# A third seven-product unit in the first product of the last two token tiles, interleaved product by product, with the sums of x taken one tile ahead

## The chip, the cores and the metric

The kernel runs on one core of a Trainium2 chip. The metric is the time of one execution on the device in microseconds. Where a profile is read, PE is the matrix engine (PEld its weight loads), DVE the vector engine, ACT the scalar engine, POOL and SP the two other engines, which here only issue transfers and do small set-up work. Each engine takes its instructions strictly in the order in which the program gave them, and waits at an instruction whose inputs or output buffer are not ready.

## The reference

Attention over pooled keys and values, and then a two-layer network with a SiLU between:

```python
k_p = k.reshape(B, H, Sp, 8, D).mean(axis=3); v_p = the same of v      # B = H = 8, S = 576, Sp = 72, D = 64
attn = softmax(q @ k_p.T / sqrt(D));  x = (attn @ v_p) as [4608, 512]
h = x @ w_in            # 512 -> 2048
g = h / (1 + exp(-h))   # SiLU
out = g @ w_out         # 2048 -> 512
```

All inputs and the output are float32; the kernel multiplies in bfloat16 and accumulates in float32.

## The kernel before

The 4608 tokens are worked in nine tiles of 512 (t = 0 to 8). A tile has two stages, written one after the other in the loop at the end of the kernel: `up` (the first product and the SiLU: x times `w_in` into `h_T`) and `down_quarters` (the second product: `h_T` times `w_out` into the output; tile 0 uses the plain `down`). The attention of batch t + 1 (scores, exponentials, denominators, numerators, and the multiplication that writes x into `xT`) is done in pieces inside tile t, and is over when tile 6 ends: tiles 7 and 8 hold only the two products.

There is no scheduler. The order on every engine is that in which the Python code runs. Each stage walks through its matmuls and calls `next(step)` before each; `spread` runs a *filler*, a small function with a due step, as soon as that step has been reached. Fillers of the first product are put into `f_up`, those of the second into `f_down`. A filler that is due at step n is issued behind the matmul of step n. Steps of `up` count one plain matmul of 512 tokens or two matmuls of 256 each; steps of `down_quarters` count one matmul (7 products of 16, 112 in all).

*The first product.* The 2048 hidden columns are 16 groups of 128. A plain group (`plain`, line 541) is four matmuls of 128x512 that accumulate in one bank, and a SiLU on ACT (line 547). Two *units* of four groups each, groups 4 to 7 and 8 to 11, are computed instead as a 2x2 block product by the seven-product method (Strassen's: seven block products of sums instead of eight of blocks). A product (`product`, line 482) is four matmuls of 128x256. The seven products use three banks P, Q and R, and are combined as they come (`stage`): 2 into P, copied by ACT into `r_sb` (line 499); 5 into Q, added on DVE to `r_sb`, giving `rr_sb` (line 502); 1 into R, from which DVE makes `t_sb` (line 505); 4 added into P and 3 added into Q, each taken by a SiLU on ACT straight from its bank; then 7 added into P and 6 added into Q, each added on DVE to `t_sb` into `c_sb[0]` and `c_sb[1]` (lines 514 and 517), which the SiLUs "h" and "s" read (line 490). So product 6 may only be issued after the SiLU of product 3 has read bank Q, and product 7 after that of product 4. `r_sb`, `rr_sb`, `t_sb` and the two `c_sb` exist once and are shared by all units. Sums of weights (`w_sum1`, five for each unit, line 442) are made once in tile 0; sums of x (`x_sum`, five for each tile, line 449) are made at the start of each tile's `up`.

In tiles 2 to 8 the order is: plain groups 12 and 13, products 2 5 1 of the first unit, group 14, products 4 3, group 15, products 7 6, and so on through the second unit with groups 0 and 1 between, ending with group 2, the SiLU s of the second unit, and group 3.

*The second product* is one seven-product unit over the whole tile. Its left operands are sums of quarters of `h_T` (`hidden_sum`, line 609, on DVE), each made in two halves of 128x1024: the half over groups 4 to 7 and 12 to 15 first, the half over groups 0 to 3 and 8 to 11 after. The order of its matmuls follows: products 2 and 5 over the first halves, products 2 and 5 over the second halves, then products 1, 4, 3, 7, 6. Product 1 needs both halves of `h_sum` 1.

PSUM has eight banks: three are handed out in turn under the tag "mm" (plain groups, R of a unit, and P, Q, R of the second product), five under "at" (scores, denominators, numerators, and P and Q of a unit). A tile that takes a bank waits until the last reader of the bank's tile before it is done. In tiles 2 to 6 `down_quarters` holds, in order: at step 56 one bank of denominators, then four of numerators, which four multiplications on DVE read (line 398); at step 75 four banks of scores (line 345), whose sixteen matmuls go round the four banks in turn; at step 97 denominators and two banks of numerators, at step 101 two more of these in tile 6.

DVE in tile 6's `down_quarters` does, in order: `rr_sb`, `hidden_sum(7)` (step 33, line 609, 128x2048), `t_sb` (line 668), four multiplications of line 398, `hidden_sum(6)` (step 71), the copy of bank Q (line 676), the addition from bank P (line 680), four more multiplications, the addition from bank Q (line 684), and then, as first work of tile 7, the five sums of x.

Of the kernel before, what the change touches and what calls it, by code (L numbers as in the profile page):

```python
# [27 lines left out]
FP32 = mybir.dt.float32  # L28
FP32R = mybir.dt.float32r
BF16 = mybir.dt.bfloat16  # L30
AX = mybir.AxisListType.X
AF = mybir.ActivationFunctionType
ALU = mybir.AluOpType
# [3 lines left out]
def kernel(  # L37
# [9 lines left out]
    nc = tc.nc  # L47

    B, H, S, D = q.shape
# [11 lines left out]
    KQ, NQ, CQ = KG // 2, NTT // 2, d_model // 2  # L61
# [20 lines left out]
    singles = ctx.enter_context(tc.tile_pool(name="singles", bufs=1))  # L82
# [8 lines left out]
    def ps_tile(shape, dtype, tag, name):  # L91
        return psum.tile(shape, dtype, tag=tag, bufs=banks[tag], name=name)
# [18 lines left out]
    t_sb = singles.tile([128, 2, CQ], FP32, name="t_sb")  # L111
    xT = singles.tile([128, KF, NX], BF16, name="xT")

    w_sum1 = [singles.tile([128, 5, 2, 256], BF16, name=f"w_sum1{n}") for n in range(2)]
    x_sum = singles.tile([128, 5, 2, NQ], BF16, name="x_sum")
    c_sb = [singles.tile([128, 2, NQ], FP32, name=f"c_sb{n}") for n in range(2)]

# [206 lines left out]
    def third(n):  # L324
        return tuple((g, n * QV, (n + 1) * QV) for g in range(2))
# [50 lines left out]
    def numerators(b, segs, tags=("at", "at")):  # L376
        st = batches[b]
        w = width(segs)
        g0, i0, i1 = segs[0]
        c0 = b * S % NX + i0 * QP  # L380
        cols = slice(c0, c0 + (i1 - i0) * QP)
        es = st.pop(("es", segs))
        rec = st.pop(("rec", segs))
        nu = []
        for c in range(2):
            nu_ps = ps_tile([128, 512], FP32, tags[c], "nu_ps")
            for g, _, _, cs in seg_cols(segs):
                for s in range(4):
                    nc.tensor.matmul(  # L389
                        nu_ps[32 * s : 32 * (s + 1), cs],  # L390
                        lhsT=st["vp"][:, 4 * g + s, c::2],
                        rhs=es[:, s, cs],
                        start=True, stop=True,
                    )
            nu.append(nu_ps)
        ng = len(segs)
        for c in range(2):
            nc.vector.tensor_mul(  # L398
                out=xT[:, 2 * g0 + c : 2 * (g0 + ng - 1) + c + 1 : 2, cols],
                in0=nu[c][:, :w].rearrange("r (g n) -> r g n", g=ng),  # L400
                in1=rec.rearrange("r (g n) -> r g n", g=ng),
            )
# [4 lines left out]
    def moe_tables():  # L407
        nc.scalar.preload_act_table_set("silu_and_others")
# [10 lines left out]

    UNITS = ((4, 6), (8, 10))
    UW = [
        {
            (i, j): w_in_sb[:, 2 * j : 2 * j + 2, 128 * u : 128 * (u + 2)]
# [7 lines left out]
    U_WI = {n: i for i, n in enumerate(U_W)}  # L433
# [6 lines left out]
    def unit_weight_sum(y, n):  # L440
        a, b = U_W[n]
        nc.vector.tensor_tensor(
            out=w_sum1[y][:, U_WI[n]], in0=UW[y][a], in1=UW[y][b],
            op=ALU.subtract if n in (6, 7) else ALU.add,
        )

    def unit_x_sum(t, n):
        a, b = U_X[n]
        nc.vector.tensor_tensor(
            out=x_sum[:, U_XI[n]], in0=x_quarter(t, *a), in1=x_quarter(t, *b),  # L450
            op=ALU.subtract if n in (3, 4) else ALU.add,
        )

    def unit_weights(y, n):
        if n in U_WI:
            return w_sum1[y][:, U_WI[n]]
        return UW[y][0, 0] if n == 3 else UW[y][1, 1]

    def unit_x(t, n):
# [5 lines left out]
    def up(t, fillers, items):  # L465
        step = spread(
            fillers,
            sum(
                KF if len(it) == 3 else 2 * len(it[1].strip("hs")) for it in items
            ),  # L470
        )
        ps = {}

        def product(y, n, bank, first):
            if first:
                tag = "mm" if bank == "R" else "at"
                ps[bank] = ps_tile([128, 2, NQ], FP32, tag, f"u_ps{bank}")
            w, x = unit_weights(y, n), unit_x(t, n)
            for u in range(2):
                next(step)  # L480
                for kk in range(2):
                    nc.tensor.matmul(  # L482
                        ps[bank][:, u, :], lhsT=w[:, kk, 128 * u : 128 * (u + 1)],
                        rhs=x[:, kk, :], start=first and u == 0 and kk == 0,
                        stop=kk == 1, skip_group_check=True,
                    )

        def hidden(y, i, j, src):
            g = UNITS[y][i]
            nc.scalar.activation(  # L490
                h_T[:, g : g + 2, j * NQ : (j + 1) * NQ], src, func=AF.Silu
            )

        tt = nc.vector.tensor_tensor

        def stage(y, n):
            if n == "2":
                product(y, 2, "P", True)
                nc.scalar.copy(r_sb, ps["P"])
            elif n == "5":  # L500
                product(y, 5, "Q", True)
                tt(out=rr_sb, in0=ps["Q"], in1=r_sb, op=ALU.add)
            elif n == "1":
                product(y, 1, "R", True)
                tt(out=t_sb, in0=ps["R"], in1=rr_sb, op=ALU.subtract)
            elif n == "4":
                product(y, 4, "P", False)
                hidden(y, 1, 0, ps["P"])
            elif n == "3":
                product(y, 3, "Q", False)  # L510
                hidden(y, 0, 1, ps["Q"])
            elif n == "7":
                product(y, 7, "P", False)
                tt(out=c_sb[0], in0=ps["P"], in1=t_sb, op=ALU.add)  # L514
            elif n == "6":
                product(y, 6, "Q", False)
                tt(out=c_sb[1], in0=ps["Q"], in1=t_sb, op=ALU.add)
            elif n == "h":
                hidden(y, 0, 0, c_sb[0])
            else:  # L520
                hidden(y, 1, 1, c_sb[1])

        for it in items:
            if len(it) == 3:
                plain(t, step, *it)
            else:
                for n in it[1]:
                    stage(it[0], n)
        for _ in step:
            pass  # L530
# [75 lines left out]
    def hidden_sum(n, k0, k1):  # L606
        a, b, op = H_SUMS[n]
        ks = slice(k0, k1)
        nc.vector.tensor_tensor(  # L609
            out=h_sum[n][:, ks, :], in0=quarter(*a, ks), in1=quarter(*b, ks), op=op  # L610
        )
# [167 lines left out]
    def load_half_2(name, half):  # L779
        for i0, i1 in ((0, SA), (SA, SLOTS), (SLOTS, SLOTS + 1)):  # L780
            load_slots(nc.gpsimd, 2, name, i0, i1, half)

    visits = [third(n) for n in range(3)]
    for t in range(NT):
        a = t + 1
        f_up, f_down = [], []
        if t == 0:
            GA = 11
            items = [(g, 0, HS) for g in range(GA)]
            items += [(g, HS, NTT - HS) for g in range(GA)]  # L790
            items += [(g, 0, NTT) for g in range(GA, KG)]
            f_up += [(1, lambda: denominators(0, part(0, 1), on_dve=True))]
            f_up += [(5, lambda: denominators(0, part(1, 1), on_dve=True))]
            f_up += [(13, lambda: numerators(0, part(0, 1)))]
            f_up += [(17, lambda: numerators(0, part(1, 1)))]
        else:
            G = lambda *gs: [(g, 0, NTT) for g in gs]
            if t == 1:
                items = (
                    G(12, 13, 14, 15) + [(0, "251")] + G(8) + [(0, "43")] + G(9)  # L800
                    + [(0, "7h6")] + G(10) + [(0, "s")] + G(11, 0, 1, 2, 3)
                )
            else:
                items = (
                    G(12, 13) + [(0, "251")] + G(14) + [(0, "43")] + G(15) + [(0, "76")]
                    + [(1, "2")] + [(0, "hs")] + [(1, "51")] + G(0) + [(1, "43")] + G(1)
                    + [(1, "7h6")] + G(2) + [(1, "s")] + G(3)
                )
            for n in U_X:
                f_up.append((0, lambda n=n: unit_x_sum(t, n)))  # L810
            for n in (2, 5):
                f_up.append((36 if t > 1 else 45, lambda n=n: hidden_sum(n, 4, 8)))
            f_up.append((56, lambda: hidden_sum(6, 4, 8)))
            for n, k0 in ((2, 0), (5, 0), (1, 4), (1, 0)):
                f_up.append((64, lambda n=n, k0=k0: hidden_sum(n, k0, k0 + 4)))
            f_down.append((33, lambda: hidden_sum(7, 0, 8)))
            f_down.append((71, lambda: hidden_sum(6, 0, 4)))
# [9 lines left out]
        if a < B:  # L827
# [50 lines left out]
            for n, sg in enumerate(visits):  # L878
                if n < 2 or not 0 < t < B - 2:
                    f_down.append((nu_at[n], lambda sg=sg: numerators(a, sg)))  # L880
                if n == 0 and 1 < t < B - 1:
                    f_down.append((nu_at[n], lambda: numerators(a - 1, visits[2])))
        moe_tables()
        up(t, f_up, items)
        if t == 0:
# [31 lines left out]
```

The softmax here doesn't subtract the row's maximum and nothing guards it: scores larger than these inputs give would overflow.

## Time and profile before

| | |
|---|---|
| median of four runs | 285.43 us (285.37 to 285.48) |
| the profiled execution | 285.24 us, of which the profile's span is 283.3 us |
| granted TensorE clock | 1.0 in all of the span |
| PE busy | 277.1 us, 98% of the span |
| DVE busy | 225.5 us, 80% |
| ACT busy | 183.5 us, 65% |
| PE's share of the chain that ended last | 91% |
| waits of PE in the chain in tiles 7 and 8, up to its last matmul | under 0.2 us each |

A busy matrix engine is read here as a queue without a gap: the start of one group of matmuls follows the start of the one before by the number of matmuls times their spacing. The ends of matmuls are modelled, some 0.17 us beyond the start of what follows, so groups overlap in the listing. The same holds for DVE and ACT in a smaller measure: back to back instructions of 0.69 us on DVE start 0.61 us apart.

### The profile page before, as it was taken

What the parts mean: (1) busy time and instruction counts of PE and PEld (TensorE: products, weight loads), DVE (VectorE), ACT (ScalarE), POOL (GpSimd) and SP (SyncE); (2) the same over time, 40 slices, a digit from 0 to 9 for tenths busy, and PEclk for the clock granted to TensorE, in tenths of its full rate; (3) what the DMA queues carried; (4) which work ended last, traced back from release to release, by engine and by line L of the source; (5) the groups of instructions that cost most, each with busy time, mean ns of one, the idle gap of its engine ahead of it and who ended that gap; (6) DMA issues with size and microseconds to landing.
All of it is one profiled execution on the core that took longest, in us unless ns stands there. A gap on an engine that the chain in (4) does not pass through costs nothing.

```text
span 283.3 us, 6909 instructions
## 1 busy us (share of the span) xinstructions
PE 277.1 (98%) x2793; PEld 194.3 (69%) x2793; DVE 225.5 (80%) x404; ACT 183.5 (65%) x359; POOL 60.8 (21%) x78
## 2 busy tenths in 40 slices
PE   8989999999999999999999999999999999999994
PEld 3338544456777677767888786687667766887684
DVE  4987836899978898879887988799888786836773
ACT  1677766568577876687668856885779467326700
POOL 8754317242140214021402130441100000000000
PEclk9999999999999999999999999999999999999999
DMA  7999998897749753986498539598830032005003
GB/s 207 287 267 226 217 307 160 235 159 127 143 62 207 168 128 47 191 186 124 68 186 183 98 82 181 126 144 115 138 97 0 2 94 56 2 18 132 1 19 132
DMA packets 31376, 37.70 MB, mean 133 GB/s; under 512 B 10352, under 2 KB 22256, under 8 KB 31344
## 3 DMA queue, kind: packets, MB, share of 16 engines
q0 software_dynamic: 23840, 26.77, 52.2%
q1 hardware_dynamic: 6928, 9.58, 12.2%
q10 hardware_dynamic: 576, 0.92, 1.0%
q8 instruction: 22, 0.36, 0.5%
q14 instruction: 10, 0.08, 0.1%
HBM read 36.70 MB, written 9.44 MB: 163 GB/s over the span
## 4 chain that ended last, share of the span: by engine, by line
PE 91%; DVE 3%; ACT 2%; DMA 2%; issue 0%; DVEq 0%
PE hp_ps L541 25%; PE o_psP L649 15%; PE o_psQ L649 15%; PE u_psP L482 7%; PE u_psQ L482 7%; PE o_psR L649 5%; PE sc_ps L345 4%; PE o_ps L576 3%; PE nu_ps L389 2%; PE u_psR L482 2%; PE den_ps L363 2%; DMA raw<-in_k_dram 2%; ACT es L353 1%; DVE w_sum L627 1%; PE warm_ps L698 1%; DVE xT L398 1%
## 5 line engine op out<-in xcount | busy, mean ns | idle before, releaser
L541 PE MATMUL hp_ps<-xT,w_in_sb 128*128 128x512 bf16 (+3 forms) x412 | 82.6, 340 | 0.5 <-ACT h_T L547 0.4
L649 PEld LDWEIGHTS <-h_sum 128*128 128x128 bf16 x640 | 60.6, 98 | 11.9 <-issue 1.3
L547 ACT ACTIVATE h_T<-hp_ps 128x512 bf16<-128x512 f32 (+2 forms) x95 | 51.3, 545 | 25.4 <-PE hp_ps L541 24.2
L541 PEld LDWEIGHTS <-w_in_sb 128*128 128x128 bf16 x412 | 39.3, 98 | 25.0 <-issue 1.4
L609 DVE TENSOR_TENSOR h_sum<-h_T 128x1024 bf16<-128x1024 bf16 (+1 forms) x72 | 50.9, 744 | 6.9 <-ACT h_T L547 6.9
L353 ACT ACTIVATE es<-sc_ps 72x384 bf16<-72x384 f32 (+1 forms) x100 | 39.0, 468 | 10.0 <-PE sc_ps L345 9.9
L482 PEld LDWEIGHTS <-w_sum 128*128 128x128 bf16 x300 | 29.3, 98 | 7.7
L649 PEld LDWEIGHTS <-h_T 128*128 128x128 bf16 x256 | 24.1, 98 | 4.4 <-issue 0.9
L398 DVE TENSOR_TENSOR xT<-nu_ps,rec 128x384 bf16<-128x384 f32 (+1 forms) x50 | 23.9, 531 | 0.2
L372 ACT ACTIVATE lnd<-den_ps 128x384 f32<-128x384 f32 (+1 forms) x23 | 11.1, 483 | 19.4 <-PE den_ps L363 19.4
L153 DVE STREAM_TRANSPOSE qT<-q_bf 128x576 bf16<-128x576 bf16 x32 | 23.0, 754 | 0.0
L490 ACT ACTIVATE h_T<-c_sb 128x512 bf16<-128x512 f32 x30 | 18.1, 626 | 5.7 <-DVE c_sb L514 5.7
L268 DVE TENSOR_TENSOR raw<-raw 128x384 f32<-128x384 f32 (+3 forms) x20 | 12.3, 617 | 8.2 <-DMA raw<-in_v_dram 4.9
L177 POOL DMA_DIRECT2D raw<-in_k_dram x5 | 7.1, 1429 | 53.3 <-DMA raw<-in_k_dram 53.3
L649 PE MATMUL o_psP<-w_out_sb,h_sum 128*128 128x256 bf16 x128 | 17.6, 273 | 0.0
L553 POOL DMA_DIRECT2D out_dram<-o_sb x1 | 0.6, 615 | 78.9 <-issue 78.9
L514 DVE TENSOR_TENSOR c_sb<-u_psP,t_sb 128x512 f32<-128x512 f32 x15 | 10.3, 689 | 8.2 <-PE u_psP L482 3.6
L649 PE MATMUL o_psQ<-w_sum,h_sum 128*128 128x256 bf16 x128 | 16.7, 273 | 0.0
L649 PE MATMUL o_psQ<-w_out_sb,h_sum 128*128 128x256 bf16 x128 | 16.6, 273 | 0.0
L649 PE MATMUL o_psP<-w_sum,h_T 128*128 128x256 bf16 x128 | 16.5, 273 | 0.0
L649 PE MATMUL o_psQ<-w_sum,h_T 128*128 128x256 bf16 x128 | 16.5, 273 | 0.0
L649 PE MATMUL o_psR<-w_sum,h_sum 128*128 128x256 bf16 x128 | 15.7, 273 | 0.0
(80 smaller groups left out, 439.5 us busy)
## 6 DMA issues: line engine op xcount, KB each, us to landing
out_dram<-o_sb SPq DMA_DIRECT2D x128, 64.0 KB, 4.2
raw<-in_k_dram POOLq DMA_DIRECT2D x10, 576.0 KB, 9.7
raw<-in_v_dram POOLq DMA_DIRECT2D x10, 576.0 KB, 7.9
q_bf<-in_q_dram POOLq DMA_DIRECT2D x6, 576.0 KB, 13.7
w_in_sb<-in_moe_w_in_dram POOLq DMA_DIRECT2D x8, 256.0 KB, 8.2
w_out_sb<-in_moe_w_out_dram POOLq DMA_DIRECT2D x4, 512.0 KB, 13.6
raw<-in_v_dram POOLq DMA_DIRECT2D x2, 768.0 KB, 11.3
raw<-in_k_dram POOLq DMA_DIRECT2D x1, 768.0 KB, 10.5
```

What stands on the lines that cost most here:

```text
L153: nc.vector.transpose(out=st["qT"][:, a, f * QF : (f + 1) * QF].rearrange("r i c p -> r (i c p)"), in_=st["q_bf"][:, a, f * n : (f + 1) * n],)
L268: nc.vector.tensor_add(out=raw[..., :w], in0=raw[..., :w], in1=raw[..., w : 2 * w])
L345: nc.tensor.matmul(sc[s][:, cs], lhsT=kz[b % 2][rows, g, c, :], rhs=st["qT"][rows, g, i0:i1, c, :], start=(c == 0), stop=(c == 1),)
L353: nc.scalar.activation(es[:, s, :], sc[s], func=AF.Exp, scale=score_scale)
L372: nc.scalar.activation(lnd, den_ps[:, :w], func=AF.Ln)
L398: nc.vector.tensor_mul(out=xT[:, 2 * g0 + c : 2 * (g0 + ng - 1) + c + 1 : 2, cols], in0=nu[c][:, :w].rearrange("r (g n) -> r g n", g=ng), ...
L482: nc.tensor.matmul(ps[bank][:, u, :], lhsT=w[:, kk, 128 * u : 128 * (u + 1)], rhs=x[:, kk, :], start=first and u == 0 and kk == 0, stop=kk ...
L490: nc.scalar.activation(h_T[:, g : g + 2, j * NQ : (j + 1) * NQ], src, func=AF.Silu)
L541: nc.tensor.matmul(hp_ps[:, r0:r1], lhsT=w_in_sb[:, kk, g * 128 : (g + 1) * 128], rhs=xT[:, kk, x0 : x0 + r1 - r0], start=(kk == 0), stop= ...
L547: nc.scalar.activation(h_T[:, g, n0 : n0 + n], hp_ps[:, :n], func=AF.Silu)
L609: nc.vector.tensor_tensor(out=h_sum[n][:, ks, :], in0=quarter(*a, ks), in1=quarter(*b, ks), op=op)
L649: nc.tensor.matmul(ps[b][:, c, :], lhsT=left(n, kt, c), rhs=W_OUT[n][:, kt, :], start=b not in begun, stop=kt == k1 - 1, skip_group_check= ...
```

## The change

Tiles 7 and 8 (`t >= B - 1`) get a third unit, over groups 12 to 15, so that only groups 0 to 3 remain plain. The order of the first product is written out in `THREE`, one string for each of the two tiles: a letter and a character name a stage of a unit (A is the new unit over groups 12 to 15, B that over 4 to 7, C that over 8 to 11; the digits are products, h and s the SiLUs from `c_sb`), g0 to g3 are plain groups. The three units are interleaved, so that one starts before the one before is finished. Banks P, Q and R are kept apart for each unit; `r_sb`, `rr_sb`, `t_sb` and `c_sb` remain shared.

The five weight sums of the new unit are made in tile 6's `down_quarters` (step 45), into two buffers that held raw keys and values at the start. The sums of x for tile 7 are made in tile 6's `down_quarters` (step 103), those for tile 8 in tile 7's (step 44), instead of at the start of each tile's `up`. The first halves of `h_sum` 2 and 5 are due at step 50 of `up` instead of 36 (`up` now has 58 steps instead of 60).

```diff
-    w_sum1 = [singles.tile([128, 5, 2, 256], BF16, name=f"w_sum1{n}") for n in range(2)]
+    w_sum1 = [
+        [w[:, i] for i in range(5)] for w in (
+            singles.tile([128, 5, 2, 256], BF16, name=f"w_sum1{n}") for n in range(2)
+        )
+    ]
...
-    UNITS = ((4, 6), (8, 10))
+    UNITS = ((4, 6), (8, 10), (12, 14))
...
-            out=w_sum1[y][:, U_WI[n]], in0=UW[y][a], in1=UW[y][b],
+            out=w_sum1[y][U_WI[n]], in0=UW[y][a], in1=UW[y][b],
...
-                ps[bank] = ps_tile([128, 2, NQ], FP32, tag, f"u_ps{bank}")
+                ps[y, bank] = ps_tile([128, 2, NQ], FP32, tag, f"u_ps{bank}")
...
+    THREE = (
+        "g0 A2 A5 g1 A4 B2 A3 A1 B5 A7 C2 A6 B4 B3 B1 C5 Ah B7 As C4 Bh B6 C1 C3 C7 Bs"
+        " C6 Ch g2 Cs g3",
+        "A2 A5 g0 A4 B2 A3 A1 B5 A7 C2 A6 B4 B3 B1 C5 Ah B7 As C4 Bh B6 C1 C3 C7 Bs g1"
+        " C6 Ch Cs g2 g3",
+    )
     visits = [third(n) for n in range(3)]
...
+            elif t >= B - 1:
+                items = []
+                for it in THREE[t - B + 1].split():
+                    items += [(("BCA".index(it[0])), it[1])] if it[0] in "ABC" else G(int(it[1]))
...
-            for n in U_X:
-                f_up.append((0, lambda n=n: unit_x_sum(t, n)))
+            if t < B - 1:
+                for n in U_X:
+                    f_up.append((0, lambda n=n: unit_x_sum(t, n)))
             for n in (2, 5):
-                f_up.append((36 if t > 1 else 45, lambda n=n: hidden_sum(n, 4, 8)))
+                h_at = 50 if t >= B - 1 else 36 if t > 1 else 45
+                f_up.append((h_at, lambda n=n: hidden_sum(n, 4, 8)))
...
+        if t in (B - 2, B - 1):
+            for n in (4, 1, 3, 7, 6):
+                f_down.append((103 if t < B - 1 else 44, lambda n=n: unit_x_sum(t + 1, n)))
+        if t == B - 2:
+            k_w = big.tile([128, 4, 2, 256], BF16, tag="k_raw2", name="w_sum12")
+            v_w = big.tile([128, 4, 2, 256], BF16, tag="v_raw2", name="w_sum12")
+            w_sum1.append([k_w[:, i] for i in range(4)] + [v_w[:, 0]])
+            for n in U_W:
+                f_down.append((45, lambda n=n: unit_weight_sum(2, n)))
         moe_tables()
         up(t, f_up, items)
```

More of the change, by code (lines that the diff above doesn't have):

```diff
@@ L455, in unit_weights @@
         if n in U_WI:
-            return w_sum1[y][:, U_WI[n]]
+            return w_sum1[y][U_WI[n]]
         return UW[y][0, 0] if n == 3 else UW[y][1, 1]
@@ L482, in product @@
                     nc.tensor.matmul(
-                        ps[bank][:, u, :], lhsT=w[:, kk, 128 * u : 128 * (u + 1)],
+                        ps[y, bank][:, u, :], lhsT=w[:, kk, 128 * u : 128 * (u + 1)],
                         rhs=x[:, kk, :], start=first and u == 0 and kk == 0,
@@ L498, in stage @@
                 product(y, 2, "P", True)
-                nc.scalar.copy(r_sb, ps["P"])
+                nc.scalar.copy(r_sb, ps[y, "P"])
             elif n == "5":
                 product(y, 5, "Q", True)
-                tt(out=rr_sb, in0=ps["Q"], in1=r_sb, op=ALU.add)
+                tt(out=rr_sb, in0=ps[y, "Q"], in1=r_sb, op=ALU.add)
             elif n == "1":
                 product(y, 1, "R", True)
-                tt(out=t_sb, in0=ps["R"], in1=rr_sb, op=ALU.subtract)
+                tt(out=t_sb, in0=ps[y, "R"], in1=rr_sb, op=ALU.subtract)
             elif n == "4":
                 product(y, 4, "P", False)
-                hidden(y, 1, 0, ps["P"])
+                hidden(y, 1, 0, ps[y, "P"])
             elif n == "3":
                 product(y, 3, "Q", False)
-                hidden(y, 0, 1, ps["Q"])
+                hidden(y, 0, 1, ps[y, "Q"])
             elif n == "7":
                 product(y, 7, "P", False)
-                tt(out=c_sb[0], in0=ps["P"], in1=t_sb, op=ALU.add)
+                tt(out=c_sb[0], in0=ps[y, "P"], in1=t_sb, op=ALU.add)
             elif n == "6":
                 product(y, 6, "Q", False)
-                tt(out=c_sb[1], in0=ps["Q"], in1=t_sb, op=ALU.add)
+                tt(out=c_sb[1], in0=ps[y, "Q"], in1=t_sb, op=ALU.add)
             elif n == "h":
```

## The prediction

> **What bounds the kernel now.** I read the table of busy time by stage first, with the stretches of tile 6, of tile 7's first product and of tile 8's (columns: stretch, its length; then PE, PEld, DVE, ACT, POOL busy with instruction counts; clock, DMA share, GB/s).
>
> ```profile
> 199.32:229.06 29.74, 29.74 (x329) 21.65 (x328) 24.57 (x41) 21.91 (x42) 0.06 (x1) 1.00 0.29 59
> 229.06:242.08 13.02, 13.02 (x91) 8.65 (x89) 9.51 (x17) 8.99 (x17) 0.00 (x0) 1.00 0.26 66
> 254.35:267.37 13.02, 13.02 (x91) 8.66 (x89) 9.51 (x17) 8.99 (x17) 0.00 (x0) 1.00 0.32 80
> ```
>
> PE is busy in the whole of each stretch, at full granted clock, and the chain of waits runs on PE through all three. So any matmul time saved is worth its full length, and any wait that PE gets costs its full length. DVE is the next: 24.57 of 29.74 us in tile 6, 9.51 of 13.02 in the others. That leaves room on average; what counts is where it is. So I next read the timeline of PE and DVE in tile 6's second product (start, length, engine, line, operation, what).
>
> ```profile
> 221.83 1.47 PE L649 MATMUL o_psQ<-w_sum,h_T 128*128 128x256 bf16 x12
> 223.24 0.53 PE L345 MATMUL sc_ps<-qT,kz 32*72 32x192 bf16 x16
> 223.70 0.61 PE L649 MATMUL o_psQ<-w_sum,h_T 128*128 128x256 bf16 x4
> ...
> 219.16 1.21 DVE L609 TENSOR_TENSOR h_sum<-h_T 128x2048 bf16<-128x2048 bf16 x1
> 220.29 0.68 DVE L668 TENSOR_TENSOR t_sb<-o_psR,rr_sb 128x512 f32<-128x512 f32 x1
> 220.89 1.93 DVE L398 TENSOR_TENSOR xT<-nu_ps,rec 128x384 bf16<-128x384 f32 x4
> ```
>
> DVE stands back to back from 219.16 to the four multiplications. Their order against the score matmuls matters: the five "at" banks go round, so after one bank of denominators and four of numerators the four banks of scores are that of the denominators and the first three of numerators. The scores may touch their fourth bank only when the third multiplication is done. Last, the same view of tile 7's first product:
>
> ```profile
> 236.72 0.69 DVE L502 TENSOR_TENSOR rr_sb<-u_psQ,r_sb 128x512 f32<-128x512 f32 x1 [0.20 <-ACT r_sb L499]
> 237.52 0.69 DVE L505 TENSOR_TENSOR t_sb<-u_psR,rr_sb 128x512 f32<-128x512 f32 x1
> 240.01 0.69 DVE L514 TENSOR_TENSOR c_sb<-u_psP,t_sb 128x512 f32<-128x512 f32 x1 [0.61 <-ACT h_T L490]
> 240.62 0.68 DVE L517 TENSOR_TENSOR c_sb<-u_psQ,t_sb 128x512 f32<-128x512 f32 x1
> 241.22 0.68 DVE L609 TENSOR_TENSOR h_sum<-h_T 128x1024 bf16<-128x1024 bf16 x1
> 242.89 2.50 DVE L609 TENSOR_TENSOR h_sum<-h_T 128x1024 bf16<-128x1024 bf16 x4 [0.99 <-ACT h_T L547]
> ...
> 238.02 0.60 PE L482 MATMUL u_psQ<-x_sum,w_in_sb 128*128 128x256 bf16 x4
> 239.32 0.60 PE L482 MATMUL u_psP<-x_sum,w_sum 128*128 128x256 bf16 x4
> 239.76 0.60 PE L482 MATMUL u_psQ<-x_sum,w_sum 128*128 128x256 bf16 x4
> 240.19 1.89 PE L541 MATMUL hp_ps<-xT,w_in_sb 128*128 128x512 bf16 x8
> ```
>
> From here come the spacings: DVE starts 0.61 apart back to back, but 0.80 where an instruction waits for the one before it (236.72 to 237.52). The four halves at the end are (2.50 - 0.68)/3 = 0.605 apart. Product 3 (238.02) and product 6 (239.76) have 1.3 us of other matmuls between them. A reader on DVE or ACT starts 0.26 after the last of four 256-column matmuls was followed up (the product of 239.32 is through at 239.76; line 514 at 240.01).
>
> **What the change saves.** Eight plain matmuls of 512 take 1.73 us in the chain, 0.216 each; a product of four takes 0.436 (239.32 to 239.76 rounded over the row of products). Sixteen plain ones (3.46) become 28 of 256 (7 x 0.436 = 3.05). That is 0.41 a tile, **0.81 us** for two, on the path.
>
> The Trainium skill, "TensorE: Matmul & The Clock Gate", section "Back-to-back issue gap", speaks against this: in streams of loads and matmuls it puts a 512-column matmul at some 131 ns and a 128-column one at some 81, so that short ones cost more a column. Halfway between, an estimate from that page, 256 columns would cost 98 ns, and the unit 28 x 98 = 2.74 against 16 x 131 = 2.10 us: 0.64 lost a tile. This trace has 216 and 109 ns, exactly in proportion, with weight loads of 98 ns under them; the measurement decides.
>
> **What it adds, at no cost.** In tiles 7 and 8 each: four more additions on DVE of 0.61 (lines 502, 505, 514, 517) and a copy on ACT of 0.58; the four SiLUs stay four. Taking the five sums of x ahead removes 1.76 from DVE there. In tile 7's second product DVE has 2.19 us idle ahead of its copy at 250.90, which hides tile 8's sums of x. In tile 6 tile 7's sums now stand ahead of line 684 (229.10), which goes 1.7 us later; behind it wait only the stores of `o_sb` on SP, whose buffer is next written some 20 us later, and the first addition of unit A, whose result has until A1's `t_sb`, 4.6 us after g0 begins (0.865 + 0.87 + 0.865 + 4 x 0.436 + 0.26). Without that slack the 1.7 would move on to A1. The weight sums have no wait of their own, since their buffers are long free, and no moved step issues a transfer.
>
> **Tile 6: the weight sums.** Five sums of 128x512 in bf16. Line 442 did ten in 3.4 us with a mean of 0.415, so (3.4 - 0.415)/9 = 0.33 apart; the sums of x give (1.76 - 0.42)/4 = 0.335. Five are 1.68 us. They stand between `hidden_sum(7)` and `t_sb`, where DVE has no gap, so all four multiplications go 1.68 later. The third starts at 220.89 + 2 x 0.46 and ends at 222.36 now; the score matmuls (16 in 0.46) reach their fourth bank at 223.24 + 3 x 0.029 = 223.33. The spare is 0.97. With 0.05 from a DVE end to a waiting PE (at the end of tile 8 DVE ends at 273.47, PE starts at 273.52), PE waits 1.68 + 0.05 - 0.97 = **0.76 us**. Bounds: 0.65 if the sums overlap with their neighbours a little more, 0.98 if the spare is a fifth of a microsecond less. Behind it nothing else is late: DVE's later work in this tile waits for PE (0.92 idle ahead of 224.34).
>
> **Tile 7: the end of the interleaving.** Count from the moment the last matmul of B1 has gone (B1 is product 1 of unit B). PE then has C5 B7 C4 B6 C1 C3 C7 C6, eight products, and g2 and g3: 8 x 0.436 + 1.73 = 5.22 until the second product begins. ACT first: C3 has gone at 2.62, its SiLU starts at 2.88 and takes 0.605 (the group of line 490 from Q), so C6 may start at 3.53, but PE is there at 3.05, with only C7 between: a wait of 0.48. DVE: `t_sb` of B at 0.26; then `rr_sb` of C (must wait for it, 0.80) at 1.06; the two `c_sb` of B at 1.67 and 2.28; `t_sb` of C 3.08 (0.80, it overwrites what the one before reads); `c_sb` of C 3.88 (0.80) and 4.49; the first half of `h_sum` 2 at 5.10, ended 5.78. PE can start the second product at 5.83 instead of 5.22: waits of **0.61** in all (the 0.48 is inside). Product 2's second half needs the fourth half-sum from there: 5.10 + 3 x 0.605 + 0.68 + 0.05 = 7.65, PE at 5.83 + 16 x 0.109 = 7.58: 0.07. Product 1 needs the seventh: 9.46, PE at 9.40: 0.06, where before 0.04 was lost too. Tile 7 loses **0.70 us**. Bounds: 0.44 if the two 0.80 that stand for an overwriting are 0.61 (ACT's 0.48 remains), 0.80 upward.
>
> **Tile 8.** There g1 stands between C7 and C6: PE needs 6.08, ACT is done in time, C6's `c_sb` starts at 4.61, the half-sum is in at 5.95. No wait, with 0.13 to spare, then 0.06 at product 2 and nothing at product 1.
>
> **Sum.** -0.81 + 0.76 + 0.70 = +0.65 us. Against the profiled execution: 285.24 + 0.65 = 285.89; the median lies 0.19 above that execution, so 286.08, told as **286.05**. About 0.57 us (0.2%) is what a measurement of this kernel can tell from no change: 284.86 to 286.00.
>
> **Rivals.**
> 1. Not slower: the weight sums are covered. Place: DVE ahead of `t_sb` in tile 6; it decides where the push on the third multiplication is under 0.97. For it: DVE is busy only 83% there. Against: the six instructions from 219.16 stand without a gap. Price: the 0.76 goes, 285.43 - 0.81 + 0.70 = 285.32, no change.
> 2. Tile 7 pays only the ACT wait (0.44), the overwriting instructions being spaced 0.61: 285.82, no change by the bound. For it: no row shows such a pair; against: the program has DVE wait for itself there.
> 3. Neither wait comes: 284.62, faster. It needs the spare in tile 6 and an earlier read of bank Q by ACT; the latter has nothing for it, with one product between C3 and C6.
> 4. Tile 8 waits as well, since its spare is 0.06 to 0.13: one more 0.19 on DVE, at two or three places, gives 0.3 to 0.5: 286.5, slower.
>
> **Numbers.** Forecast 0.44 (its own range 285.75 to 286.35, three quarters of it above 286.00), rival 1 0.17, rival 2 0.15, rival 3 0.11, rival 4 0.13. Slower: 0.33 + 0.13 + 0.02 of rival 2 = 0.48; faster: 0.11; within the bound the rest, 0.41. The range 285.2 to 286.6 leaves out rival 3, a corner of rival 1 and the end of rival 4.
>
> **What would show it.** A wait of PE of about 0.75 in the scores of tile 6's third visit, released by line 402 (398 before); a wait of about 0.46 before C6 released by ACT; a short one ahead of the second product of tile 7 released by `h_sum`; no such in tile 8; 28 products at 0.436 in place of 16 plain matmuls at 0.216. I am wrong if DVE reaches `t_sb` of tile 6 early, or if C6 starts without a gap.

## The result and the profile after

The changed kernel takes 286.07 us (median of 32 runs; before 285.43, of 50 runs). The ratio is 1.0022, with a 95% interval of 1.0017 to 1.0028: slower by 0.64 us. The interval leaves 1 out, though the difference is just over the 0.2% at which the prediction drew the line. The profiled execution took 286.07 us, its span is 284.2 us.

Busy time by stage of the kernel after, with the stretches of tile 6, of tile 7's first product and of tile 8's (columns as in the table of before):

```profile
199.46:229.91 30.45, 30.11 (x329) 21.72 (x327) 26.30 (x47) 21.86 (x42) 0.21 (x1) 1.00 0.31 58
229.91:243.10 13.19, 12.89 (x103) 9.68 (x100) 10.65 (x20) 9.41 (x19) 0.00 (x0) 1.00 0.26 66
...
255.46:268.08 12.62, 12.62 (x103) 9.79 (x100) 9.38 (x15) 9.44 (x18) 0.00 (x0) 1.00 0.33 85
```

(The first stretch begins 0.11 us behind tile 6's first matmul; counted from that one, tile 6 is 229.91 - 199.35 = 30.56 us long, and 29.74 before.) Three things are to be seen. Tile 8's first product has PE busy all through and is 12.62 us long, where it was 13.02: the saved matmul time, in full. Tile 7's has 0.30 us in which PE is not busy and is 13.19 long: longer than before, although it holds the same shorter work. And tile 6, whose matmuls are unchanged, has 0.34 us of idle PE where it had none. (That is less than PE lost there, 0.82 us by the length of the tile: a score matmul counts as busy for its modelled 0.24 us, though the next can start 0.029 after it.)

Here is tile 6's second product in the timeline of the kernel after, PE and then DVE:

```profile
223.44 0.62 PE L349 MATMUL sc_ps<-qT,kz 32*72 32x192 bf16 x3
224.29 0.49 PE L349 MATMUL sc_ps<-qT,kz 32*72 32x192 bf16 x13 [0.23 <-DVE xT L402]
224.71 0.61 PE L653 MATMUL o_psQ<-w_sum,h_T 128*128 128x256 bf16 x4
...
219.36 1.21 DVE L613 TENSOR_TENSOR h_sum<-h_T 128x2048 bf16<-128x2048 bf16 x1
220.49 1.75 DVE L446 TENSOR_TENSOR w_sum<-w_in_sb 128x512 bf16<-128x512 bf16 x5
222.17 0.68 DVE L672 TENSOR_TENSOR t_sb<-o_psR,rr_sb 128x512 f32<-128x512 f32 x1
222.77 1.93 DVE L402 TENSOR_TENSOR xT<-nu_ps,rec 128x384 bf16<-128x384 f32 x4
```

Sixteen score matmuls that took 0.46 us in one piece are cut after the first three: the fourth bank comes only with the third multiplication, and all four multiplications stand behind five weight sums that take 1.68 us on DVE. What followed the scores starts 1.27 us after them (223.44 to 224.71) where it was 0.46: PE lost 0.81 us.

And the end of tile 7's first product, PE, DVE, then ACT:

```profile
239.50 0.60 PE L486 MATMUL u_psQ<-x_sum,w_in_sb 128*128 128x256 bf16 x4
239.93 0.60 PE L486 MATMUL u_psP<-x_sum,w_sum 128*128 128x256 bf16 x4
240.83 0.60 PE L486 MATMUL u_psQ<-x_sum,w_sum 128*128 128x256 bf16 x4 [0.30 <-ACT h_T L494]
241.26 1.89 PE L545 MATMUL hp_ps<-xT,w_in_sb 128*128 128x512 bf16 x8
243.10 1.05 PE L653 MATMUL o_psP<-w_out_sb,h_sum 128*128 128x256 bf16 x8
...
239.54 0.68 DVE L521 TENSOR_TENSOR c_sb<-u_psQ,t_sb 128x512 f32<-128x512 f32 x1
240.33 0.69 DVE L509 TENSOR_TENSOR t_sb<-u_psR,rr_sb 128x512 f32<-128x512 f32 x1
241.16 0.69 DVE L518 TENSOR_TENSOR c_sb<-u_psP,t_sb 128x512 f32<-128x512 f32 x1
241.76 0.68 DVE L521 TENSOR_TENSOR c_sb<-u_psQ,t_sb 128x512 f32<-128x512 f32 x1
242.36 3.09 DVE L613 TENSOR_TENSOR h_sum<-h_T 128x1024 bf16<-128x1024 bf16 x5
...
240.20 0.58 ACT L494 ACTIVATE h_T<-u_psQ 128x512 bf16<-128x512 f32 x1
```

The first line is product 3 of the last unit (C3), the second C7, the third C6. C6 has to wait until ACT has read C3's bank: it starts 0.90 after C7 instead of 0.436, a wait of 0.46. (The listing gives 0.30 in its bracket, since it counts from the modelled end of the matmul before, some 0.17 after the next could have started.) From 241.26 two plain groups need 1.73, so PE could begin the second product at 242.99, and begins at 243.10: the first half-sum starts on DVE at 242.36, takes 0.68, and PE follows 0.06 later. DVE has waited for no other engine since 237.51.

### The profile page after: what moved, and what is told of

Same layout as the page of the kernel before. It is cut to its first block, busy times and chain, and to the rows that moved or that the text cites. A ratio compares the mean times of both kernels' runs of the same rounds, so it can differ in the third digit from the quotient of the medians.

```text
span 284.2 us, 6976 instructions
## 1 busy us (share of the span) xinstructions
PE 277.3 (98%) x2817; PEld 196.9 (69%) x2817; DVE 232.0 (82%) x417; ACT 184.6 (65%) x361; POOL 60.6 (21%) x78
## 4 chain that ended last, share of the span: by engine, by line
PE 87%; DVE 6%; ACT 4%; issue 2%; DVEq 0%
PE hp_ps L545 22%; PE o_psQ L653 14%; PE o_psP L653 14%; PE u_psQ L486 7%; PE u_psP L486 7%; PE o_psR L653 5%; PE sc_ps L349 4%; PE o_ps L580 3%; PE warm_ps L702 3%; PE u_psR L486 2%; PE nu_ps L393 2%; PE den_ps L367 2%; DVE xT L402 1%; ACT es L357 1%; DVE h_sum L613 1%
## 5 line engine op out<-in xcount | busy, mean ns | idle before, releaser
L545 PE MATMUL hp_ps<-xT,w_in_sb 128*128 128x512 bf16 (+3 forms) x380 | 74.7, 337 | 0.5 <-ACT h_T L551 0.4
L551 ACT ACTIVATE h_T<-hp_ps 128x512 bf16<-128x512 f32 (+2 forms) x87 | 46.5, 541 | 19.2 <-PE hp_ps L545 18.0
L545 PEld LDWEIGHTS <-w_in_sb 128*128 128x128 bf16 x380 | 36.2, 98 | 22.5 <-issue 1.4
L486 PEld LDWEIGHTS <-w_sum 128*128 128x128 bf16 x340 | 33.3, 98 | 7.7 <-issue 0.5
L494 ACT ACTIVATE h_T<-c_sb 128x512 bf16<-128x512 f32 x34 | 20.6, 626 | 5.7 <-DVE c_sb L518 5.6
L503 ACT COPY r_sb<-u_psP 128x512 f32<-128x512 f32 x17 | 9.9, 584 | 10.2 <-PE u_psP L486 7.6
L509 DVE TENSOR_TENSOR t_sb<-u_psR,rr_sb 128x512 f32<-128x512 f32 x17 | 11.8, 692 | 5.8 <-PE u_psR L486 4.1
```

The lines of the kernel that those rows point to most:

```text
L486: nc.tensor.matmul(ps[y, bank][:, u, :], lhsT=w[:, kk, 128 * u : 128 * (u + 1)], rhs=x[:, kk, :], start=first and u == 0 and kk == 0, stop ...
L494: nc.scalar.activation(h_T[:, g : g + 2, j * NQ : (j + 1) * NQ], src, func=AF.Silu)
L509: tt(out=t_sb, in0=ps[y, "R"], in1=rr_sb, op=ALU.subtract)
L545: nc.tensor.matmul(hp_ps[:, r0:r1], lhsT=w_in_sb[:, kk, g * 128 : (g + 1) * 128], rhs=xT[:, kk, x0 : x0 + r1 - r0], start=(kk == 0), stop= ...
L551: nc.scalar.activation(h_T[:, g, n0 : n0 + n], hp_ps[:, :n], func=AF.Silu)
```

## The experiments

Each kernel is the one after with the edit shown, unless it says otherwise. Since a few tenths of a microsecond are at issue, two numbers stand for each: the median with the ratio's interval against runs of the kernel before on the same chip, and a stretch of the profile, from the start of tile 6's first matmul to the start of the last group of matmuls. That stretch holds all that the change touches, and leaves out the first 50 us, where profiles differ by up to 0.8 us at places that no edit touches. (Of `best`, four of the weight sums lie ahead of it, in tiles 2 to 5; they cost nothing there: from tile 1's plain groups to tile 6 it takes 199.19 - 52.13 = 147.06 us, before 199.16 - 52.03 = 147.13.)

| kernel | median us | ratio, 95% interval | stretch us | against before |
|---|---|---|---|---|
| before | 285.43 | 1 | 278.75 - 199.16 = 79.59 | |
| after | 286.07 | 1.0022 (1.0017 to 1.0028) | 279.62 - 199.35 = 80.27 | +0.68 |
| sumsonly | 286.18 | 1.0028 (1.0018 to 1.0037) | 279.81 - 199.40 = 80.41 | +0.82 |
| w82 | 285.18 | 0.999 (0.9981 to 1.0) | 278.44 - 198.98 = 79.46 | -0.13 |
| t8only | 285.04 | 0.9987 (0.9978 to 0.9997) | 278.94 - 199.73 = 79.21 | -0.38 |
| c3first | 285.9 | 1.002 (1.0008 to 1.0033) | 279.50 - 199.22 = 80.28 | +0.69 |
| split | 285.78 | 1.0013 (1.0005 to 1.0022) | 279.29 - 199.26 = 80.03 | +0.44 |
| c3split | 285.44 | 1.0006 (0.9996 to 1.0017) | 279.79 - 199.71 = 80.08 | +0.49 |
| no_lead | 284.98 | 0.9986 (0.9978 to 0.9995) | 278.30 - 198.94 = 79.36 | -0.23 |
| best | 284.31 | 0.996 (0.9947 to 0.9974) | 277.87 - 199.19 = 78.68 | -0.91 |

The medians of the experiments are of 11 or 12 executions each, that of best of 5. Taken against the kernel before on the same chip (285.41 and 285.42), they differ from what the stretches give by up to 0.21 us, and in c3split by 0.47.

### Tile 6: the weight sums alone (sumsonly), and moved (w82)

`sumsonly` is the kernel before, with the five weight sums added at the change's place, and nothing reading them:

```diff
+            for n in U_W:
+                f_down.append((45, lambda n=n: unit_weight_sum(2, n)))
```

> The kernel before with one thing of the change added: the five weight sums at step 45 of tile 6's second product, whose results nothing reads; no third unit, sums of x where they were. My theory: PE waits 0.75 to 0.85 us in the third score visit of tile 6 and nowhere else, 285.43 + 0.8 = 286.23. Rival, that the 1.7 us on DVE are covered as DVE is busy only 83% of that tile: 285.43. Second rival, that part of the wait came from the sums of x moved ahead or from the new order behind it: between 285.5 and 285.9.

Measured: 286.18 us; the stretch is 0.82 longer. Its PE timeline in tile 6, and the group with which tile 7 begins:

```profile
223.48 0.63 PE L349 MATMUL sc_ps<-qT,kz 32*72 32x192 bf16 x3
224.34 0.48 PE L349 MATMUL sc_ps<-qT,kz 32*72 32x192 bf16 x13 [0.23 <-DVE xT L402]
...
229.96 1.89 PE L545 MATMUL hp_ps<-xT,w_in_sb 128*128 128x512 bf16 x8
```

The same cut after three matmuls, and tile 6 is 229.96 - 199.40 = 30.56 us long, as with the whole change (229.91 - 199.35), where it was 228.90 - 199.16 = 29.74. So the weight sums cost 0.82 us without the third unit, the new order or the moved sums of x.

`w82` leaves the change whole and moves the same five sums behind the copy of bank Q:

```diff
-                f_down.append((45, lambda n=n: unit_weight_sum(2, n)))
+                f_down.append((82, lambda n=n: unit_weight_sum(2, n)))
```

> The changed kernel with the five weight sums of the new unit due at step 82 of tile 6's second product instead of 45, so behind the copy of bank Q, where DVE waits for PE (0.92 and 1.11 us idle in the profile of before). My theory, that the sums push the multiplications in front of the third score visit: PE's wait in these scores (0.81 us measured with the change) goes, nothing takes its place, 286.07 - 0.8 = 285.27. Rival, that the scores would have waited for something else at the same place (the exponentials on ACT, the denominators' bank): the time stays at 286.0 to 286.1.

Measured: 285.18 us, the stretch 0.13 shorter than before the change. In its timeline the scores are in one piece, and the sums stand on DVE behind a wait for PE:

```profile
223.07 0.53 PE L349 MATMUL sc_ps<-qT,kz 32*72 32x192 bf16 x16
...
224.18 0.69 DVE L680 COPY o_sb<-o_psQ 128x512 f32<-128x512 f32 x1 [0.92 <-PE o_psQ L653]
224.78 1.76 DVE L446 TENSOR_TENSOR w_sum<-w_in_sb 128x512 bf16<-128x512 bf16 x5
226.46 0.69 DVE L684 TENSOR_TENSOR o_sb<-o_psP,t_sb 128x512 f32<-128x512 f32 x1
```

The same work on the same engine in the same tile costs PE nothing here, and 0.8 us where it stood.

### The unit in tile 8 alone (t8only)

```diff
-            elif t >= B - 1:
+            elif t >= B:
...
-            if t < B - 1:
+            if t < B:
```

with the sums of x ahead for tile 8 only, the half-sums at step 50 in tile 8 only, and the weight sums at step 82.

> The third unit in tile 8 alone, in the order that the change gives tile 8; tile 7 as before; the five weight sums at step 82 of tile 6's second product. My theory: tile 8 gains its 0.41 us in full and nothing is lost, 285.43 - 0.41 = 285.02. Rival, that DVE binds at the end of tile 8's first product too: 285.2 to 285.5.

Measured: 285.04 us, the stretch 0.38 shorter. No wait of PE over 0.2 us is left in the chain of tiles 7 and 8, so the unit does give its 0.4 us a tile where the order leaves room.

### Tile 7: which wait sets the end (c3first, split, c3split)

Two waits stand in tile 7, one on ACT (C6) and one on DVE (the first half-sum). `c3first` takes the one on ACT away, by issuing C3 and its SiLU earlier:

```diff
-        "g0 A2 A5 g1 A4 B2 A3 A1 B5 A7 C2 A6 B4 B3 B1 C5 Ah B7 As C4 Bh B6 C1 C3 C7 Bs"
+        "g0 A2 A5 g1 A4 B2 A3 A1 B5 A7 C2 A6 B4 B3 B1 C5 Ah B7 As C4 B6 C3 Bh C1 C7 Bs"
         " C6 Ch g2 Cs g3",
```

> The changed kernel with one thing in tile 7's order moved: product 3 of the last unit (C3) ahead of Bh and C1, so that its SiLU is read out of bank Q before product 6 (C6) comes, and ACT no longer makes PE wait there. My theory, that the DVE chain from B1 to the second product sets the end of this stage whatever ACT does: the wait of 0.46 us before C6 goes, and a wait of about 0.55 us (0.11 before) appears at the start of tile 7's second product; no gain, 286.0 to 286.1. Rival, that ACT's read of bank Q is the loss: 0.4 us gained, 285.65.

`split` leaves the order and gives the middle unit an `rr_sb` and a `t_sb` of its own, so that DVE doesn't overwrite what its instruction just before reads or writes:

```diff
+            rr_b, t_b = second if second and y == 0 else (rr_sb, t_sb)
...
-                tt(out=rr_sb, in0=ps[y, "Q"], in1=r_sb, op=ALU.add)
+                tt(out=rr_b, in0=ps[y, "Q"], in1=r_sb, op=ALU.add)
...
```

The lines left out put `rr_b` and `t_b` in the same way wherever `rr_sb` and `t_sb` stood, and take the two second buffers from one that held raw keys, so the listing calls both of them `raw`.

> The changed kernel with a second rr_sb and t_sb for the middle unit of tiles 7 and 8, so that DVE need not wait for its own instruction before overwriting (0.80 us apart becomes 0.61 at two places between B1 and the second product); the order and ACT as in the change. My theory: ACT's wait of 0.46 us before C6 now stands alone, no wait at the start of tile 7's second product, nor at its product 2; tile 7 loses 0.45 instead of 0.68 us, 286.07 - 0.23 = 285.84. Rival, that those spacings are not due to the overwriting: the DVE instructions stay 0.80 apart and the time at 286.05.

`c3split` has both edits.

> Both of the two edits above: C3 ahead, and a second rr_sb and t_sb. My theory: neither ACT nor overwriting, but C1 now comes one product later, so the DVE chain still ends 0.40 us behind PE at the start of the second product, and two short waits follow: tile 7 loses about 0.5 us, 285.85 to 285.9. Rival, that ACT's wait is the only loss: no wait over 0.1 us in tile 7, 285.4.

PE's timeline at the start of the second product, c3first:

```profile
240.70 1.89 PE L545 MATMUL hp_ps<-xT,w_in_sb 128*128 128x512 bf16 x8
242.98 1.05 PE L653 MATMUL o_psP<-w_out_sb,h_sum 128*128 128x256 bf16 x8 [0.38 <-DVE h_sum L613]
```

The wait on ACT is gone, and the one on DVE has grown to 242.98 - 240.70 - 1.73 = 0.55: tile 7's first product lasts 242.98 - 229.79 = 13.19 us, to the hundredth as long as with the wait on ACT. Now split, PE and DVE:

```profile
240.69 0.60 PE L488 MATMUL u_psQ<-x_sum,w_sum 128*128 128x256 bf16 x4 [0.25 <-ACT h_T L496]
241.12 1.89 PE L548 MATMUL hp_ps<-xT,w_in_sb 128*128 128x512 bf16 x8
242.85 1.04 PE L656 MATMUL o_psP<-w_out_sb,h_sum 128*128 128x256 bf16 x8
...
237.42 0.69 DVE L512 TENSOR_TENSOR raw<-u_psR,raw 128x512 f32<-128x512 f32 x1 [0.55 <-PE u_psR L488]
238.03 0.68 DVE L509 TENSOR_TENSOR rr_sb<-u_psQ,r_sb 128x512 f32<-128x512 f32 x1
...
239.24 0.69 DVE L524 TENSOR_TENSOR c_sb<-u_psQ,raw 128x512 f32<-128x512 f32 x1
239.85 0.68 DVE L512 TENSOR_TENSOR t_sb<-u_psR,rr_sb 128x512 f32<-128x512 f32 x1
```

`rr_sb` follows 0.61 after the instruction before it (0.83 in the kernel after, 237.51 to 238.34), and `t_sb` 0.61 (0.79, 239.54 to 240.33). The second product starts as soon as the plain groups are through (241.12 + 1.73 = 242.85); what is left is ACT's wait, now 0.41. The stretch is 0.24 shorter than with the change; the expectation said 0.23. In c3split PE and DVE stand as follows:

```profile
241.17 1.89 PE L548 MATMUL hp_ps<-xT,w_in_sb 128*128 128x512 bf16 x8
243.27 1.05 PE L656 MATMUL o_psP<-w_out_sb,h_sum 128*128 128x256 bf16 x8 [0.21 <-DVE h_sum L616]
...
239.86 0.60 PE L488 MATMUL u_psR<-x_sum,w_sum 128*128 128x256 bf16 x4
240.30 0.60 PE L488 MATMUL u_psP<-x_sum,w_sum 128*128 128x256 bf16 x4
...
239.69 0.69 DVE L524 TENSOR_TENSOR c_sb<-u_psQ,raw 128x512 f32<-128x512 f32 x1
240.50 0.69 DVE L512 TENSOR_TENSOR t_sb<-u_psR,rr_sb 128x512 f32<-128x512 f32 x1
```

There the wait on DVE is 243.27 - 241.17 - 1.73 = 0.37 and the stretch 0.19 shorter than with the change, as expected. C1, which writes `u_psR`, now stands behind C3 and is through at 240.30; `t_sb` starts 0.20 later, the same delay after a product into R as where the listing names PE as what DVE waits for (in the kernel after: through at 237.31, `t_sb` at 237.51). So DVE starts `t_sb` 0.81 after the instruction before it for another reason, a late C1.

The median of c3split doesn't settle this: 285.44 is the number of the rival (285.4), and the theory said 285.85 to 285.9. Its eleven executions fall into two groups, six from 285.19 to 285.44 and five from 285.99 to 286.22; the profiled one, 286.18, is of the second. The groups lie about as far apart as profiles differ in the first 50 us (0.8), but whether that is the reason was not shown. The rival falls by the profile, which has the wait that it denies.

By the stretches the kernels stand as the DVE chain has it: with ACT's wait taken away the one on DVE sets the end (c3first), with the overwriting taken away the one on ACT does (split), and with both edits the one on DVE again, because C1 has moved (c3split).

### The cover of the sums of x (no_lead)

```diff
-        "g0 A2 A5 g1 A4 B2 A3 A1 B5 A7 C2 A6 B4 B3 B1 C5 Ah B7 As C4 Bh B6 C1 C3 C7 Bs"
-        " C6 Ch g2 Cs g3",
+        "A2 A5 g0 A4 B2 A3 A1 B5 A7 C2 A6 B4 B3 B1 C5 Ah B7 As C4 Bh B6 C1 C3 C7 Bs g1"
+        " C6 Ch Cs g2 g3",
```

for tile 7, with the weight sums at step 82.

> The weight sums at step 82 of tile 6's second product, and tile 7 in the order that the change gives tile 8 (a plain group between products 7 and 6 of the last unit, but only one plain group among the first products instead of two); the sums of x for tile 7 still in front of the last addition of tile 6. This takes away the cover that I named for the sums of x. My theory: nothing at the end of tile 7's first product any more, but the first addition of unit A comes late behind the sums, and PE waits 0.5 to 0.85 us for it at A3 (bank Q): 285.1 to 285.45. Rival, that the sums of x ahead cost nothing anywhere: no wait, 284.6.

Measured: 284.98 us, the stretch 0.23 shorter than before the change. The timeline at the start of tile 7, PE and DVE:

```profile
230.86 0.60 PE L486 MATMUL u_psP<-xT,w_sum 128*128 128x256 bf16 x4
231.88 0.60 PE L486 MATMUL u_psQ<-x_sum,w_in_sb 128*128 128x256 bf16 x4 [0.42 <-DVE rr_sb L506]
...
228.87 1.75 DVE L453 TENSOR_TENSOR x_sum<-xT 128x512 bf16<-128x512 bf16 x5
230.55 0.68 DVE L688 TENSOR_TENSOR o_sb<-o_psQ,t_sb 128x512 f32<-128x512 f32 x1
231.15 0.68 DVE L506 TENSOR_TENSOR rr_sb<-u_psQ,r_sb 128x512 f32<-128x512 f32 x1
```

A3 waits 231.88 - 230.86 - 0.436 = 0.58 us for `rr_sb`, which stands behind the sums of x and the addition of tile 6. That wait is in the expected range, and -0.81 + 0.58 is the -0.23 of the stretch; the median lies 0.12 under the expected 285.1 to 285.45. The end of tile 7's first product is free of waits here. So the lead of two plain groups that the change gives tile 7 is what hides the sums of x, and it is taken from the end, where it is missed.

### A version without either loss (best)

```diff
-                f_down.append((103 if t < B - 1 else 44, lambda n=n: unit_x_sum(t + 1, n)))
-        if t == B - 2:
+                f_down.append((82 if t < B - 1 else 44, lambda n=n: unit_x_sum(t + 1, n)))
+        if t == 2:
...
-            for n in U_W:
-                f_down.append((45, lambda n=n: unit_weight_sum(2, n)))
+        if 2 <= t < 2 + 5:
+            f_down.append((82, lambda n=list(U_W)[t - 2]: unit_weight_sum(2, n)))
```

with tile 7 in tile 8's order.

> Third unit in both tiles, with both losses taken away: the five weight sums one by one in the second products of tiles 2 to 6 at step 82, the sums of x for tile 7 at step 82 of tile 6's second product (all of tile 7's x is written by then), and tile 7 in the order that the change gives tile 8, with a plain group between products 7 and 6 of the last unit. My theory: the saved matmul time of 0.81 us is seen in full, 285.43 - 0.81 = 284.62, and no wait of PE over 0.1 us in tiles 6 and 7. Rival, that three interleaved units in tile 7 overload DVE whatever the order: a wait of 0.4 to 0.7 us at the start of tile 7's second product, 285.0 to 285.3.

Measured: 284.31 us, the median of five executions, a ratio of 0.996 (0.9947 to 0.9974) to the kernel before: faster than both. It is 0.3 below the forecast 284.62, and the stretch accounts for 0.1 of that. PE at the end of tile 7's first product:

```profile
238.00 0.60 PE L486 MATMUL u_psP<-x_sum,w_sum 128*128 128x256 bf16 x4
238.43 1.03 PE L545 MATMUL hp_ps<-xT,w_in_sb 128*128 128x512 bf16 x4
239.30 0.60 PE L486 MATMUL u_psQ<-x_sum,w_sum 128*128 128x256 bf16 x4
239.73 1.89 PE L545 MATMUL hp_ps<-xT,w_in_sb 128*128 128x512 bf16 x8
241.46 1.04 PE L653 MATMUL o_psP<-w_out_sb,h_sum 128*128 128x256 bf16 x8
```

No gap: the plain group between C7 and C6 gives ACT its time, and it gives DVE 0.865 us more before the second product begins. (Two plain groups stand behind C6 here as in the kernel after.) The stretch is 0.91 shorter, 0.1 more than the matmuls saved; tile 6 there is 228.84 - 199.19 = 29.65 us, 0.09 shorter than before. The difference stands at the denominators ahead of the second score visit: before, the scores start 216.83 - 216.46 = 0.37 behind them, here 216.76 - 216.49 = 0.27, and the last exponential on ACT, which the denominators read, is over at 216.21 instead of 216.53. Why ACT is ahead there stays open.

## Why the prediction was right

- *The sum.* Forecast +0.65, 286.05 us; measured +0.64, 286.07, and +0.68 in the stretch. That the sum agrees to 0.03 is in part luck: tile 6 cost 0.06 more than forecast and tile 7 0.04 less. The prediction gave "slower" no more than 0.48.
- *The saving of 0.81.* Tile 8 went from 13.02 to 12.62 us; t8only gained 0.38 by the stretch, best 0.91. The products stand 0.436 apart in the kernel after too. By the prediction's estimate from the prices in the Trainium skill's page "TensorE: Matmul & The Clock Gate", section "Back-to-back issue gap", the third unit would have been a loss of 0.64 us a tile; tile 8 alone shows that it isn't one here. (The 98 ns of that estimate is interpolated by columns, a third of the way from the 128-column price to the 512-column one, and not halfway.)
- *Tile 6, 0.76.* 0.82 by the length of the tile, and the same with the sums alone. The spacing on DVE was as taken: the five sums put `t_sb` back by 1.68 (220.49 to 222.17). The wait for the fourth bank was 0.76 as forecast (224.29 instead of 223.44 + 3 x 0.029 = 223.53); the thirteen matmuls behind it then took 0.42 (224.29 to 224.71), where 13 x 0.029 would be 0.38. (The bound of 0.98 should have been 0.96, 0.76 and a fifth of a microsecond.) The rival that had them covered, as DVE is busy 83% of the tile, fell with sumsonly.
- *Tile 7, 0.70.* From the start of the tile to product 1 of the second product it is 246.71 - 229.91 = 16.80 us, before 245.45 - 228.90 = 16.55. So 0.25 longer with 0.41 less of matmuls: 0.66 lost, of which 0.58 ahead of the second product (forecast 0.61). The steps of the DVE chain came as counted, from 0.20 after B1 was through (237.31 to 237.51) instead of 0.26, to the half-sum at 5.05 instead of 5.10. The rival with ACT's wait alone (0.44) is what split makes of the kernel, not what the change does.
- *Tile 8, nothing.* No wait; the rival with one more in tile 8 fell.
- *The sums of x at no cost.* The cost was right and the cover too, the lead of two plain groups; the limit was misplaced. The prediction gave the first addition of unit A until A1's `t_sb`, 4.6 us after g0 begins. But that addition reads bank Q, into which A3 adds, so A3 is what waits for it, 0.865 + 0.872 + 0.865 + 2 x 0.436 = 3.47 us after g0 begins. With the change `rr_sb` is over at 232.08 + 0.69 = 232.77 and A3 starts at 233.38, so the spare was about 0.6 us. Without the lead it was A3 that waited, 0.58, and not A1.

## What to carry to other kernels

Where one engine is busy all the time, work added to another engine is priced by its place and not by that engine's share: look for the instruction behind it whose result or bank the busy engine takes next, and count the spare of that one. If there is no spare, move the work behind a wait that the second engine has anyway. Where two waits end at nearly the same time, taking away the one that the profile names may gain nothing; write down both chains to the next common point before choosing, and keep filler work of the busy engine (here the plain groups) for the place where both are long.

## What the runs showed that I had not expected

- The same instructions reached tile 6 at 198.94 to 199.73 us of the span, and the plain groups of tile 1 at 51.82 to 52.59, so the spread arises in the first 50 us; there DVE waits for the loads of keys and values (7.9 us in the kernel before), but which wait makes the spread was not shown. It is larger than the effect under study. From tile 6 on, two kernels that by the theory should agree did to 0.01 us (80.27 and 80.28 for after and c3first).
- That an overwriting instruction pays like a waiting one was taken by the prediction without a row. The runs show it: a DVE instruction that overwrites what the instruction just before it reads starts 0.79 to 0.83 us after that one, instead of 0.61, and the extra 0.2 is gone with a second buffer (split). Two such places made 0.24 us, against a result of 0.64, and no listing names them as a wait.
